# Written order for the first transform and the start of the first chunk

## The chip, the cores and the metric

One core of a Trainium2 chip runs the whole kernel as one program. The metric is the device time of one execution in microseconds. The core has five queues that matter here: TensorE (PE, with its weight loads as PEld), VectorE (DVE), ScalarE (ACT), GpSimd (POOL) and SyncE (SP), which only issues DMAs. Each executes its own instructions in order and waits on semaphores for the others.

## The reference

Eight sequences of 3072 tokens with 256 channels go through three stages:

```python
y = irfft(rfft(x, axis=1) * (filt_r + 1j*filt_i), n=3072, axis=1)
xk, xr = mix of y and y shifted by one token, with mu_k and mu_r
k = relu(xk @ w_k); v = (k*k) @ w_v; r = sigmoid(xr @ w_r); z = r * v
h = max(z @ w1, z @ w2, z @ w3); out = h @ w_out
```

The weights arrive as 64-bit floats. Most products are made from a high and a low part of each factor, as three matmuls.

## The kernel before

The long transform is cut in two factors, 48 x 64. `fft_first` does it for sequence 0, where nothing else is there to overlap with; `fft(b)` yields the pieces of the transform of sequence b, which `drive` mixes into the work of the sequence before. `fft_first` has two loops. Stage A (16 steps) multiplies x by `wa_f` and stores the result to `s1` in DRAM (`evac`, L474 and L475, on the SP queue). Stage B/C (12 steps, and two to drain) reads `s1` back (`x_load`), multiplies (tile `pb`), and makes two products with the filter (tile names in the profile: `filt` for the DVE product at L547, `q` for the POOL product at L544 from the half-swapped copy `v`, L542 and L543). Two steps later it multiplies again (`pc`) and stores to `s2` (L474, on the ACT queue). `w_double` copies halves of the matrices `wcr` and `wci` (L462, L463). The DVE product is written over the filter `f`, so it waits until POOL has read `f`.

`y_load(i)` reads one chunk of `s2` (a sequence has 8 chunks): tile `cin`, and `cprev` for the first. `y_mm(i)` finishes the inverse transform (`py`), copies it to `yt` and mixes it with the token before (`xm`, L606 on ACT and L607 on DVE), splits it in two parts (`xh`, `xl`), for `k` and `r`. `kv(i)` yields the units of one chunk: `k_mm` (`pk`), `v_mm` (`pv`, which takes `w_v` pieces of tile `ws` through `piece_of`), `r_mm`, and `y_load` and `y_mm` of the next chunk. After four chunks `second(0)` starts on w1, w2, w3 and w_out.

Weights are narrowed by jobs. `piece` gives each job a load (`wst`, three buffers, L201) and a narrowing: one ACT instruction (`we`, L212), five DVE instructions (L213 to L219) and a POOL addition (`wf`, L222). `parts` then makes the high part (DVE L231, or ACT L229 if `late`) and the low part (POOL L232). `wjobs1` holds nine jobs: 0 to 3 for `w_k`, 4 to 7 for `w_v` (their parts go to `wvd` in DRAM by a POOL-issued DMA, L273, and come back as `ws`), 8 for `w_r`. `wjobs2` holds twelve: nine for w1, w2 and w3, three for `w_out`; the nine have sums made by matmuls (`ps`), stored to `wud`. `pipelined` makes step k load job k+1, narrow job k and finish job k-2; these steps are inserted among the units of the first chunks.

What sets the order: a planner that estimates times puts the instructions of each engine in order, except inside `manual_schedule`, where the instructions of the named engines keep the order in which they are written among themselves. Instructions written outside of it may still be put ahead. Before the change SP keeps its order until `y_load(0)`, and ACT and PE for `fft_first`; DVE and POOL are left to the planner throughout. Jobs 0 to 4 are narrowed in `fft_first`, each whole at one step (`CONV`); jobs 5 to 8 are written behind `y_mm(0)`.

Of the kernel before, what the change touches and what calls it, by code (L numbers as in the profile page):

```python
# [9 lines left out]
F32 = mybir.dt.float32  # L10
F32R = mybir.dt.float32r
I32 = mybir.dt.int32
U32 = mybir.dt.uint32
# [112 lines left out]
def tile_spectral_moe(ctx: ExitStack, tc, x, filt, ones, wa, wa1, wi, wbc, wb1, wc1, filt1, filt0, mu, w_k, w_v, w_r, w1, w2, w3, w_out, out):  # L126
# [57 lines left out]
    def piece(src, kt, t0, t1, c0, c1, parts):  # L184

        wide = src.dtype != F32
        if wide:
            src = src.bitcast(I32)
        v = src.rearrange("(t p) n -> p t n", p=P)
        a, c = t1 - t0, c1 - c0  # L190
        st = {}

        def load(stage=None):
            if stage is not None:
                st["t"] = stage.rearrange("p (a n) -> p a n", a=a)
# [7 lines left out]
        def narrow(late=True):  # L203
            if not wide:
                st["r"] = st["t"]
                return
# [5 lines left out]
            nc.scalar.activation(ef, high.bitcast(F32), AF.Abs)  # L212
            nc.vector.tensor_scalar(ef, ef, as_float(0x38000000), as_float(0x47EFFFFF), op0=ALU.max, op1=ALU.min)  # L213
            nc.vector.tensor_scalar(e, e, 3, 0x3FFFFFFF, op0=ALU.logical_shift_left, op1=ALU.bitwise_and)
            nc.vector.scalar_tensor_tensor(e, high, -0x40000000, e, ALU.bitwise_and, ALU.bitwise_or)
            m = fp.tile([P, a, c], I32, tag="fin", name="wm")
            mf = m.bitcast(F32)
            nc.vector.tensor_scalar(m, e, -0x800000, None, op0=ALU.bitwise_and)
            nc.vector.scalar_tensor_tensor(mf, low.bitcast(U32), 2.0**-52, mf, ALU.mult, ALU.mult)  # L219
            cnt[0] += 1  # L220
            r = fp.tile([P, a, c], F32, tag=("flo", "fhi")[cnt[0] % 2], name="wf")
            nc.gpsimd.tensor_tensor(r, ef, mf, ALU.add)  # L222
            st["r"] = r

        return load, narrow, lambda late=True: parts(st["r"], late)

    def to_parts(hi, lo, r, late):
        if late:
# [194 lines left out]
    def fft_first(pp, jobs):  # L423
# [59 lines left out]
        xb = []  # L483

        def x_load(s):
# [24 lines left out]
        w_double(0)  # L510
        f_load(3)
        jobs[1][0]()
        x_load(1)
        wb_load(1)
        wc_load(1)
        f_load(4)
        jobs[2][0]()
        f_load(5)
        x_load(2)
        stage = pp.tile([P, 2, 1024 if wide else 512], I32 if wide else F32, tag="big", name="stage", bufs=4)  # L520
        jobs[3][0]()
        f_load(6)
        qs = {}
        for s in range(NG // 2 + 2):
            if 7 <= s + 4 < NG // 2:
                f_load(s + 4)
            if s == 4:
                wb_load(2)
                w_double(1)
            if s == 6:  # L530
                wc_load(2)
            if s in LOAD:
                jobs[LOAD[s]][0](*((stage[:, LOAD[s] - 4],) if LOAD[s] < 6 else ()))
            if s < NG // 2:
                p = ps.tile([NK, 2, C], F32, tag="pm", name="pb")
                for k in range(2):
                    g = 2 * s + k
                    mm(p[:, k], wt[g // LW][0][:, g % LW], xb[g // LX][:, g % LX], True, True)
                f = ft[s]
                q = pp.tile([NK, 2, C], F32, tag="q1", name="q1", bufs=3)  # L540
# [7 lines left out]
                qs[s] = q  # L548
            if s >= 2:
                f, q = ft[s - 2], qs[s - 2]  # L550
                p = ps.tile([NK, 2, C], F32, tag="pm", name="pc")
                for k in range(2):
                    g = 2 * (s - 2) + k
# [7 lines left out]
            if s == 8:  # L561
                w_double(2)

    first = ExitStack()
    first.enter_context(tc.manual_schedule(engines={mybir.EngineType.SP}))
# [303 lines left out]
    eye = mp.tile([P, 2, P], F32, tag="osb", name="eye")  # L869
    nc.sync.dma_start(eye, ones)  # L870
    for k in (5, 6, 7, 8):
        wjobs1[k][1]()
        wjobs1[k][2]()
    NPAIR = NTOT // 2
    units = kv(0) + kv(1) + kv(2) + [(0.0, lambda: combos(0))] + kv(3)
    marks, cuts = {}, {}
    before2 = len(units)
    s, left = second(0)
# [25 lines left out]
    lead = before2 + n2  # L904
    starts = [0] + [marks[b] + n2 for b in range(1, B)]
    ends = starts[1:] + [len(units)]
    for b in range(B):
        part = units[starts[b] : ends[b]]
        if b + 1 < B:
            side = fft(b + 1)  # L910
            cut = cuts[b] + n2 - starts[b]
            if b == 0:
                for _, fn in part[:lead]:
                    fn()
                part, cut = part[lead:], cut - lead
# [52 lines left out]
```

## Time and profile before

| | |
|---|---|
| Median of three runs | 3201.74 us (3200.74 to 3212.22) |
| Profiled execution, its own time | 3198.21 us |
| Its span | 3196.4 us |
| PE matmul busy | 3105.7 us (97%) |
| DVE, ACT, POOL busy | 1784.9, 1913.8, 1864.1 us |

Times below are microseconds from the start of the span of the profiled execution. The page cuts the span in 40 slices of 80 us; matmuls fill 6 and 7 tenths of the first two slices and 9 tenths or more of all from the third but the last. Everything that the change edits runs in the first three slices. PE busy time is modelled at the ends of matmuls, so small idle stretches are better read from the starts of instructions.

### The profile page before, as it was taken

To read this page: it belongs to the slowest core of one execution; us is meant where nothing else is said; L and a number is where in the kernel's file an instruction comes from. 1 tells how busy PE (TensorE), PEld (TensorE's weight loads), DVE (VectorE), ACT (ScalarE), POOL (GpSimd) and SP (SyncE) were. 2 spreads that over 40 slices of the span, in tenths; PEclk is the share of its full clock that TensorE was granted. 3 is DMA by queue.
4 is the path that set the end of the run, shared out by engine and by line. 5 is a ranking of instruction groups with operands and counts; after the bars stand their busy time and mean duration, and the time that the engine had idled before them with its cause. 6 is when DMAs were issued, how large, how long until landed. Compare 5 with 4: busy or idle time off the path is not lost.

```text
span 3196.4 us, 55749 instructions
## 1 busy us (share of the span) xinstructions
PE 3105.7 (97%) x19256; PEld 3031.7 (95%) x19256; DVE 1784.9 (56%) x2882; ACT 1913.8 (60%) x4024; POOL 1864.1 (58%) x1619
## 2 busy tenths in 40 slices
PE   6799999999999999999999999999999999999998
PEld 4789999999999999999999999999999999999998
DVE  4865564456554665456645466446664456555554
ACT  5556556656666566656666566665666566655554
POOL 3545675567655676546666566566665567544443
PEclk9899999999999999999999999999999999999999
DMA  8767796657766676757766577665876667555553
GB/s 292 234 227 226 235 329 192 195 181 247 246 197 184 213 241 211 215 173 234 257 198 186 178 259 252 198 191 165 269 249 189 190 195 245 182 170 160 166 168 122
DMA packets 397783, 676.38 MB, mean 212 GB/s; under 512 B 41920, under 2 KB 153664, under 8 KB 396864
## 3 DMA queue, kind: packets, MB, share of 16 engines
q1 hardware_dynamic: 328336, 585.61, 58.4%
q10 hardware_dynamic: 66752, 78.75, 7.2%
q0 software_dynamic: 2416, 8.46, 0.8%
q8 instruction: 156, 2.56, 0.3%
q14 instruction: 123, 1.01, 0.1%
HBM read 580.51 MB, written 92.14 MB: 210 GB/s over the span
## 4 chain that ended last, share of the span: by engine, by line
PE 84%; DMA 6%; DVE 5%; issue 2%; ACT 2%; POOL 1%; ACTq 0%; SPq 0%; POOLq 0%; DVEq 0%
PE pb L153 19%; PE pk L153 14%; PE pv L153 14%; PE po L153 12%; PE pe L153 9%; PE pa L153 7%; PE pr L153 4%; PE py L153 3%; DMA ws<-wud 3%; PE pc L153 2%; DVE xm L607 1%; DMA xb<-s 1%; PE ps L153 1%; DVE sc L665 1%; DVE m L748 1%
## 5 line engine op out<-in xcount | busy, mean ns | idle before, releaser
L153 PE MATMUL pb<-x,ws 128*128 128x384 f32 x3456 | 753.1, 338 | 23.0 <-DMA ws<-wud 16.9
L179 POOL TENSOR_TENSOR hh<-m,hh 128x384 fp32r<-128x384 f32 x384 | 402.2, 1056 | 522.4 <-ACT hh L178 426.3
L179 POOL TENSOR_TENSOR klo<-kr,khi 128x384 fp32r<-128x384 f32 x492 | 515.8, 1058 | 231.6 <-ACT khi L178 218.7
L153 PEld LDWEIGHTS pb<-x,ws 128*128 128x128 f32 x3456 | 598.7, 188 | 39.0 <-issue 15.2
L633 DVE SCALAR_TENSOR_TENSOR kr<-pk,kr 128x384 f32<-128x384 f32 x512 | 280.7, 553 | 444.9 <-ACT kr L632 443.6
L153 PE MATMUL po<-wo_hi,hh 128*128 128x256 f32 x2304 | 481.0, 283 | 3.1 <-ACT hh L178 1.6
L153 PE MATMUL pv<-khi,ws 128*128 128x384 f32 x2048 | 474.6, 337 | 4.0 <-ACT khi L178 4.0
L153 PEld LDWEIGHTS po<-wo_hi,hh 128*128 128x128 f32 x2304 | 389.9, 190 | 7.6 <-ACT hh L178 4.0
L153 PE MATMUL pe<-x,ws 128*128 128x384 f32 x1728 | 389.0, 337 | 0.6
L178 ACT CAST khi<-kr 128x384 fp32r<-128x384 f32 x512 | 260.2, 513 | 185.0 <-DVE kr L633 167.6
L153 PEld LDWEIGHTS pv<-khi,ws 128*128 128x128 f32 x2048 | 360.4, 188 | 7.0 <-ACT khi L178 5.3
L153 PE MATMUL pk<-xh,wk_hi 128*128 128x384 f32 x1024 | 341.4, 338 | 7.6 <-ACT xh L178 6.2
L153 PE MATMUL pk<-xl,wk_hi 128*128 128x384 f32 x1024 | 343.6, 336 | 0.9 <-DVE xl L179 0.9
L153 PE MATMUL pk<-xh,wk_lo 128*128 128x384 f32 x1024 | 343.4, 335 | 0.0
L153 PE MATMUL po<-wo_lo,hh 128*128 128x256 f32 x1152 | 316.6, 282 | 0.0
L632 ACT ACTIVATE kr<-pk 128x384 f32<-128x384 f32 x512 | 249.9, 490 | 109.0 <-POOL klo L179 48.7
L748 DVE TENSOR_TENSOR m<-sc,m 128x384 f32<-128x384 f32 x384 | 307.8, 806 | 9.2
L153 PEld LDWEIGHTS pe<-x,ws 128*128 128x128 f32 x1728 | 296.0, 188 | 3.1 <-PE pb L153 2.2
L153 PE MATMUL pv<-klo,ws 128*128 128x384 f32 x1024 | 292.3, 337 | 0.8 <-POOL klo L179 0.4
L179 POOL TENSOR_TENSOR xl<-xm,xh 128x768 fp32r<-128x768 f32 x126 | 233.4, 1869 | 89.7 <-ACT xh L178 89.7
L178 ACT CAST hh<-m 128x384 fp32r<-128x384 f32 x384 | 193.0, 514 | 134.2 <-DVE m L748 67.0
L607 DVE SCALAR_TENSOR_TENSOR xm<-yt,nmu_s,xm 128x384 f32<-128x384 f32 x256 | 180.1, 748 | 145.4 <-ACT xm L606 145.4
(129 smaller groups left out, 6028.0 us busy)
## 6 DMA issues: line engine op xcount, KB each, us to landing
ws<-wud SPq DMA_DIRECT2D x864, 256.0 KB, 3.5
ws<-wvd SPq DMA_DIRECT2D x512, 256.0 KB, 3.3
filt<-in_filt SPq DMA_DIRECT2D x84, 512.0 KB, 5.3
ws<-wud SPq DMA_DIRECT2D x288, 128.0 KB, 3.5
wbc<-wbcd SPq DMA_DIRECT2D x72, 512.0 KB, 5.4
cin<-s SPq DMA_DIRECT2D x64, 384.0 KB, 4.2
out_dram<-osb ACTq DMA_DIRECT2D x192, 128.0 KB, 3.1
xb<-s SPq DMA_DIRECT2D x85, 256.0 KB, 3.5
```

Source lines behind the costliest of these rows:

```text
L153: nc.tensor.matmul(o, lhsT=wgt, rhs=rhs, start=start, stop=stop, skip_group_check=more)
L178: nc.scalar.copy(hi, src)
L179: (lo_eng or nc.gpsimd).tensor_tensor(lo, src, hi.bitcast(F32), ALU.subtract)
L607: nc.vector.scalar_tensor_tensor(v[:, h], yt[:, h, :, :MC], nmu_s[:, w, h : h + 1], v[:, h], ALU.mult, ALU.add)
L632: nc.scalar.activation(r, p, AF.Relu)
L633: nc.vector.scalar_tensor_tensor(r, p, 0.0, r, ALU.max, ALU.mult)
L665: eng.tensor_tensor(t, a, b, ALU.subtract)
L748: nc.vector.tensor_tensor(m, c, m, ALU.max)
```

## The change

`piece` gains `steps`, a list of the single instructions of a narrowing with its parts as the last entry. `fft_first` collects such steps in `todo` and takes three of them (four from step 8 on) at the end of each step of stage B/C. The DVE product goes to a buffer of its own, `u`, instead of over `f`. `x_load(0)` moves ahead of the filter and `wc` loads; the loads of jobs 3 to 8 stand at steps 2 and 8 to 12. Jobs 5 and 6 are narrowed ahead of `y_load(0)`, jobs 7 and 8 behind `y_mm(0)`. ACT, PE, DVE and POOL keep the written order until then. The first eight `ws` loads (`piece_of(0)`) are written there, and SP keeps its written order until twelve units of the first chunks have been written.

```diff
-        CONV = {0: 1, 3: 2, 5: 3, 8: 4}
-        LOAD = {6: 4, 8: 5, 9: 6, 11: 7}
+        LOAD = {2: 3, 8: 4, 9: 5, 10: 6, 11: 7, 12: 8}
+        CONV = {2: 1, 5: 2, 8: 3, 11: 4}
...
+        def convert(n):
+            while todo and n:
+                todo.pop(0)()
+                n -= 1
...
-            if s == 4:
-                nc.sync.dma_start(f0, filt0)
-                f_load(0)
             if s == 6:
-                wc_load(0)
-                jobs[0][1](False)
-                jobs[0][2](False)
+                todo += jobs[0][3]()
+        convert(8)
+        x_load(0)
+        nc.sync.dma_start(f0, filt0)
+        f_load(0)
+        wc_load(0)
         f_load(1)
+        x_load(1)
+        jobs[1][0]()
         f_load(2)
-        x_load(0)
-        w_double(0)
...
+                nc.vector.scalar_tensor_tensor(u, p, sgn, f, ALU.mult, ALU.mult)
                 nc.scalar.copy(v[:H], p[H:])
                 nc.scalar.copy(v[H:], p[:H])
                 nc.gpsimd.tensor_tensor(q, v, f, ALU.mult)
-                nc.vector.scalar_tensor_tensor(f, p, sgn, f, ALU.mult, ALU.mult)
...
+            if s in (1, 4, 8):
+                w_double((1, 4, 8).index(s))
...
             if s in CONV:
-                k = CONV[s]
-                jobs[k][1](False)
-                jobs[k][2](False)
+                todo += jobs[CONV[s]][3]()
+            convert(3 if s < 8 else 4)
+        convert(len(todo))
...
-    with tc.tile_pool(name="pp", bufs=1) as pp, tc.manual_schedule(
-        engines={mybir.EngineType.Activation, mybir.EngineType.PE}
-    ):
+    start = ExitStack()
+    start.enter_context(tc.manual_schedule(engines={ET.Activation, ET.PE, ET.DVE, ET.Pool}))
+    with tc.tile_pool(name="pp", bufs=1) as pp:
         fft_first(pp, wjobs1)
...
+    for k in (5, 6):
+        for fn in wjobs1[k][3](True):
+            fn()
     y_load(0)
-    first.close()
...
-    wjobs1[8][0]()
     y_mm(0)
-    for k in (5, 6, 7, 8):
-        wjobs1[k][1]()
-        wjobs1[k][2]()
+    for k in (7, 8):
+        for fn in wjobs1[k][3](True):
+            fn()
+    chunk0 = kv(0)
+    piece_of(0)
+    start.close()
...
+    FIRST = 12
+    for _, fn in units[:FIRST]:
+        fn()
+    first.close()
```

## Rows read from the trace of the kernel before

**Rows 1.** Busy time by stage; in brackets instructions, then granted clock, DMA share, GB/s.

```profile
28.00:62.00 34.00, 22.40 (x84) 17.49 (x84) 15.14 (x21) 17.17 (x26) 15.01 (x12) 0.80 0.99 342
62.00:86.00 24.00, 17.46 (x70) 13.67 (x68) 20.11 (x27) 15.60 (x26) 17.30 (x13) 0.93 0.55 192
86.00:98.00 12.00, 0.00 (x0) 0.00 (x0) 11.48 (x15) 3.08 (x6) 8.54 (x8) 0.64 1.02 327
98.00:113.50 15.50, 10.26 (x37) 9.54 (x38) 15.29 (x26) 6.99 (x15) 5.13 (x4) 0.51 0.91 310
...
138.00:197.00 59.00, 57.72 (x397) 56.87 (x396) 50.78 (x78) 36.30 (x74) 30.46 (x24) 1.00 0.61 203
```

**Rows 2.** Chain of waits up to 130 us: start, duration, what.

```profile
33.29 11.17 DMA wb<-in_wb
44.47 10.16 DMA filt<-in_filt
...
76.98 1.40 DVE wm L218
```

**Rows 3.** Timeline of the SP queue: start, duration, line, transfer.

```profile
83.21 0.37 SPq L201 DMA_DIRECT2D wst<-in_w  x1
...
90.07 0.38 SPq L201 DMA_DIRECT2D wst<-in_w  x1
90.67 0.68 SPq L579 DMA_DIRECT2D cin<-s  x1
```

**Rows 4.** Timeline of stage B/C: its first and twelfth step, its last store.

```profile
34.78 2.05 PE L153 MATMUL pb<-xb,wb 128*128 128x256 f32 x4 [9.88 <-DMA xb<-s]
...
71.03 1.03 PE L153 MATMUL pb<-xb,wb 128*128 128x256 f32 x4
...
85.55 0.33 ACTq L475 DMA_DIRECT2D s<-e  x1
```

**Rows 5.** Groups of instructions by line and form, 28 to 86 us.

```profile
L544 POOL TENSOR_TENSOR q<-v,filt 128x512 f32<-128x512 f32 x12 | 16.7, 1394 | 22.2 <-ACT v L543 22.0
L547 DVE SCALAR_TENSOR_TENSOR filt<-pb,sgn,filt 128x512 f32<-128x512 f32 x12 | 8.9, 744 | 21.7 <-POOL q L544 21.7
L222 POOL TENSOR_TENSOR wf<-we,wm 128x512 f32<-128x512 f32 x6 | 8.1, 1349 | 3.8 <-DVE wm L219 3.8
L474 ACT COPY e<-pc 128x512 f32<-128x512 f32 x12 | 7.0, 585 | 7.0 <-PE pc L153 6.8
L542 ACT COPY v<-pb 64x512 f32<-64x512 f32 x12 | 7.0, 582 | 14.5 <-PE pb L153 7.1 <-PE pc L153 3.4 <-POOL wf L222 2.1
```

**Rows 6.** One tile's instructions up to 240 us: duration in ns, minimum/median/maximum.

```profile
L213 DVE TENSOR_SCALAR we<-we x21: 412/427/1351, 20.1 to 193.7; 128x512 f32<-128x512 f32 x21
L215 DVE SCALAR_TENSOR_TENSOR we<-wst,we x19: 676/691/1783, 21.0 to 196.1; 128x512 int32<-128x512 int32 x19
```

**Rows 7.** The page's DMA issues: count, KB each, median us to landing.

```profile
cin<-s SPq DMA_DIRECT2D x64, 384.0 KB, 4.2
```

**Rows 8.** DMA issues between 75 and 100 us.

```profile
wvd<-wvs POOLq DMA_DIRECT2D x4, 512.0 KB, 4.5
...
s<-e ACTq DMA_DIRECT2D x3, 256.0 KB, 4.7
```

**Rows 9.** Timeline from the first `py` to the first `pk`.

```profile
98.10 3.70 PE L153 MATMUL py<-wi_s,cin 96*128 96x96 f32 x16 [12.18 <-DMA eye<-in_ones]
...
105.71 3.21 DVE L607 SCALAR_TENSOR_TENSOR xm<-yt,nmu_s,xm 128x384 f32<-128x384 f32 x4
...
106.92 1.65 PE L153 MATMUL pk<-xh,wk_hi 128*128 128x384 f32 x4 [4.27 <-ACT xh L178]
```

**Rows 10.** Timeline of later narrowings and of the last `ps`.

```profile
134.47 0.43 DVE L213 TENSOR_SCALAR we<-we 128x512 f32<-128x512 f32 x1 [0.99 <-ACT we L212]
...
193.71 0.43 DVE L213 TENSOR_SCALAR we<-we 128x512 f32<-128x512 f32 x1 [3.10 <-ACT we L212]
...
210.24 1.72 PE L153 MATMUL ps<-wf,eye 128*128 128x128 f32 x14
```

More of the change, by code (lines that the diff above doesn't have):

```diff
@@ L201, in load, with steps @@
             nc.sync.dma_start(st["t"], v[:, t0:t1, k * c0 : k * c1])
-        def narrow(late=True):
+        def steps(late=False):
             if not wide:
                 st["r"] = st["t"]
-                return
+                return [lambda: parts(st["r"], late)]
             w = st["t"].rearrange("p a (n k) -> p a n k", k=2)
@@ L211, in narrow, with add, split_up @@
             ef = e.bitcast(F32)
[L212 to L215, printed above, removed]
             m = fp.tile([P, a, c], I32, tag="fin", name="wm")
             mf = m.bitcast(F32)
[L218 to L225, printed above, removed]
+            vec = nc.vector
+            def add():
+                cnt[0] += 1
+                r = fp.tile([P, a, c], F32, tag=("flo", "fhi")[cnt[0] % 2], name="wf")
+                nc.gpsimd.tensor_tensor(r, ef, mf, ALU.add)
+                st["r"] = r
+            return [
+                lambda: nc.scalar.activation(ef, high.bitcast(F32), AF.Abs),
+                lambda: vec.tensor_scalar(ef, ef, as_float(0x38000000), as_float(0x47EFFFFF), op0=ALU.max, op1=ALU.min),
+                lambda: vec.tensor_scalar(e, e, 3, 0x3FFFFFFF, op0=ALU.logical_shift_left, op1=ALU.bitwise_and),
+                lambda: vec.scalar_tensor_tensor(e, high, -0x40000000, e, ALU.bitwise_and, ALU.bitwise_or),
+                lambda: vec.tensor_scalar(m, e, -0x800000, None, op0=ALU.bitwise_and),
+                lambda: vec.scalar_tensor_tensor(mf, low.bitcast(U32), 2.0**-52, mf, ALU.mult, ALU.mult),
+                add,
+                lambda: parts(st["r"], late),
+            ]
+        def narrow():
+            for fn in steps()[:-1]:
+                fn()
+        def split_up(late=True):
+            if not wide:
+                st["r"] = st["t"]
+            parts(st["r"], late)
+        return load, narrow, split_up, steps
     def to_parts(hi, lo, r, late):
@@ L517, in fft_first @@
         jobs[2][0]()
+        x_load(2)
         f_load(5)
-        x_load(2)
+        f_load(6)
         stage = pp.tile([P, 2, 1024 if wide else 512], I32 if wide else F32, tag="big", name="stage", bufs=4)
-        jobs[3][0]()
-        f_load(6)
         qs = {}
@@ L528, in fft_first @@
                 wb_load(2)
-                w_double(1)
             if s == 6:
@@ L532, in fft_first @@
             if s in LOAD:
-                jobs[LOAD[s]][0](*((stage[:, LOAD[s] - 4],) if LOAD[s] < 6 else ()))
+                jobs[LOAD[s]][0](*((stage[:, LOAD[s] - 4],) if 4 <= LOAD[s] < 6 else ()))
             if s < NG // 2:
@@ L539, in fft_first @@
                 f = ft[s]
+                u = pp.tile([NK, 2, C], F32, tag="u1", name="u1", bufs=3)
                 q = pp.tile([NK, 2, C], F32, tag="q1", name="q1", bufs=3)
                 v = pp.tile([NK, 2, C], F32, tag="v1", name="v1", bufs=2)
+                nc.vector.scalar_tensor_tensor(u, p, sgn, f, ALU.mult, ALU.mult)
                 nc.scalar.copy(v[:H], p[H:])
@@ L546, in fft_first @@
                     nc.gpsimd.tensor_tensor(q[:H, 0], v[:H, 0], f0, ALU.mult)
[L547 to L548 removed]
+                qs[s] = u, q
+            if s in (1, 4, 8):
+                w_double((1, 4, 8).index(s))
             if s >= 2:
[L550 removed]
+                f, q = qs[s - 2]
                 p = ps.tile([NK, 2, C], F32, tag="pm", name="pc")
@@ L557, in fft_first @@
             if s in CONV:
-                k = CONV[s]
-                jobs[k][1](False)
-                jobs[k][2](False)
-            if s == 8:
-                w_double(2)
-    first = ExitStack()
-    first.enter_context(tc.manual_schedule(engines={mybir.EngineType.SP}))
-    with tc.tile_pool(name="pp", bufs=1) as pp, tc.manual_schedule(
-        engines={mybir.EngineType.Activation, mybir.EngineType.PE}
-    ):
+                todo += jobs[CONV[s]][3]()
+            convert(3 if s < 8 else 4)
+        convert(len(todo))
+    first = ExitStack()
+    ET = mybir.EngineType
+    first.enter_context(tc.manual_schedule(engines={ET.SP}))
+    start = ExitStack()
+    start.enter_context(tc.manual_schedule(engines={ET.Activation, ET.PE, ET.DVE, ET.Pool}))
+    with tc.tile_pool(name="pp", bufs=1) as pp:
         fft_first(pp, wjobs1)
@@ L858, in second @@
         return u, [(0.71, lambda q=q: o_mm(p, NU // 2 - 1, q)) for q in range(2 * NTB)]
+    for k in (5, 6):
+        for fn in wjobs1[k][3](True):
+            fn()
     y_load(0)
-    first.close()
+    eye = mp.tile([P, 2, P], F32, tag="osb", name="eye")
+    nc.sync.dma_start(eye, ones)
     for _ in range(8):
@@ L866, in tile_spectral_moe @@
         mm(p, wk[0][:, 0, :P], wk[0][:, 0, :NT], True, True)
-    wjobs1[8][0]()
     y_mm(0)
-    eye = mp.tile([P, 2, P], F32, tag="osb", name="eye")
-    nc.sync.dma_start(eye, ones)
-    for k in (5, 6, 7, 8):
-        wjobs1[k][1]()
-        wjobs1[k][2]()
+    for k in (7, 8):
[4 more added lines that the diff above has]
+    start.close()
     NPAIR = NTOT // 2
-    units = kv(0) + kv(1) + kv(2) + [(0.0, lambda: combos(0))] + kv(3)
+    units = chunk0 + kv(1) + kv(2) + [(0.0, lambda: combos(0))] + kv(3)
     marks, cuts = {}, {}
@@ L906, in tile_spectral_moe @@
     ends = starts[1:] + [len(units)]
+    FIRST = 12
+    for _, fn in units[:FIRST]:
+        fn()
+    first.close()
+    starts[0] = FIRST
     for b in range(B):
@@ L912, in tile_spectral_moe @@
             if b == 0:
-                for _, fn in part[:lead]:
+                for _, fn in part[: lead - FIRST]:
                     fn()
-                part, cut = part[lead:], cut - lead
+                part, cut = part[lead - FIRST :], cut - lead + FIRST
             drive(part[:cut], side, sum(w for w, _ in part[:cut]), sum(w for w, _ in side))
```

3 lines of the change are left out of this document (1 added, 2 removed).

## The prediction, made before the changed kernel was run

> **What bounds the kernel now.** I read the page's slices first: matmuls fill nine tenths of every slice from the third on, so the change can only move the moment at which that dense part begins, or disturb it. The table by stage comes next [rows 1]. From 28 to 62 us the DMA engines are full (share 0.99, 342 GB/s) while every compute engine has room: the first transform is bound by its loads there. The chain of waits agrees: it runs through a load of `wb` and one of `filt` [rows 2]. From 62 to 86 us the DMA share is 0.55 and DVE is busy 20.11 of 24 us [rows 1]; the chain now goes from one narrowing instruction to the next [rows 2], though what has to be finished is the transform. From 86 to 98 us PE does nothing and DVE is busy 11.48 of 12 us [rows 1]. The matmuls wait for `cin`, whose load is issued at 90.67 and whose result is used at 98.10 [rows 3, 9]. From 98 to 113.5 us the granted clock is 0.51, so TensorE runs at the lower of its two levels, after it had stood idle; from 138 us it is 1.00 and PE is busy 57.72 of 59 us [rows 1]. There DVE is the next engine, with 50.78 of 59.
>
> **The stage B/C loop.** Now it takes its first `pb` at 34.78, its twelfth at 71.03 and issues its last store at 85.55 [rows 4]: 36.25 us for eleven steps, 3.30 each, and a tail of 14.5 us.
>
> Ahead of `x_load(0)` go away `f0` (64 KB), one filter piece (256 KB) and the two halves of `wc` (256 KB each), 0.85 MB by their tile shapes. At 342 GB/s [rows 1] that is 2.5 us, so the first `pb` comes at about 32.3. The bounds are 0 and 2.5; I take the whole, because the queue is full there. The same bytes are behind it now, and steps 2 to 4 wait for them, so this alone would be worth less than 2.5 at the end of the loop.
>
> Per step ACT has three copies, 0.58 + 0.58 + 0.59 us [rows 5], and a store issue of 0.33 [rows 4]. My estimate for the ACT shares of four narrowings and of six `w_double` copies, spread over twelve steps, is 0.7; I took an ACT narrowing instruction like a copy of its size and a `w_double` copy, twice as wide, at twice that: (4 x 0.6 + 6 x 1.05) / 12. Sum 2.8 us. POOL has 1.39 for `q`, and per job 1.35 for the sum and about the same for the low part [rows 5], a third of that per step: 2.3 us. DVE has 0.74 for `u` [rows 5] and a third of a job: 3 x 0.43 + 2 x 0.69 for the narrowing [rows 6] and 0.43 for the high part, 3.1 per job, so 1.03 per step. The narrowing instructions take 0.43 alone and up to 1.35 when they meet POOL, those with two inputs 0.69 and up to 1.78 [rows 6]. If they and POOL never run together, the step takes 2.3 + 1.03 = 3.3 us. DMA gives a bound too: from `x_load(0)` to the last filter piece 12.7 MB have to pass (x 3.1, filter 3.2, `wb` 1.0, `wc` 1.6, jobs 1 to 3 1.6, eight stores 2.1), 37 us at 342 GB/s, hence a little over 3 us per step. I take 3.15, between 2.8 and 3.5: the twelfth `pb` at 32.3 + 11 x 3.15 = 67.
>
> The tail shortens for two reasons. Jobs 5 and 6 no longer stand between its instructions, and `u` needs no wait for `q`: the wait of `filt` for POOL, 21.7 us in this stretch [rows 5], goes. What is late next is `q`, which ACT feeds. From the last `pb`: 1.0 for it, 1.2 for two copies, 1.4 for `q`, 2.0 for `pc` (eight matmuls, where the four of `pb` take 1.03 [rows 4]), 0.6 for the copy and 0.5 to the issue, 6.7 us. The last store goes out at 73.7 instead of 85.55: **-12 us** (bounds: 2.8 per step gives -16, 3.5 and a tail of 8 gives -7).
>
> **From the last store to `py`.** Now 12.55 us (85.55 to 98.10) [rows 4, 9]. `cin` is issued 0.6 after a `wst` load that the planner had put ahead and that waited for a buffer [rows 3], and it then shares full DMA engines (1.02) [rows 1]. In the new order nothing of the second job list is ahead of it. The store may land in 3.5 us (median here 4.7 [rows 8]), `cin` and `cprev` take 1.4 to issue and 4.2 to land [rows 7]: 9.1 us, **-3.5** (bounds 0 and -5). The narrowing of jobs 5 and 6 is hidden in this stretch: two times 3.1 us of DVE and two times 2.7 of POOL in 9 us. Without that cover it would hold up `y_mm(0)` by the excess.
>
> **`y_mm(0)`.** DVE takes up `xm` at 105.71, 7.6 us after `py` [rows 9], because narrowings stood before it. In the written order it is free. But ACT and DVE then alternate for each half, where the planner had put four ACT instructions side by side. I expect the first half of `xh` 1 us sooner after `py`: **-1** (bounds -2 and +2).
>
> **What is given back.** Two things. First, `piece_of(0)` writes eight `ws` loads into SP's fixed order, and the last two need job 7, which is narrowed only behind `y_mm(0)`. SP stands in front of them, and behind it stand `cin` of the second chunk and the first loads of the second job list. From the start of `py`: 6 us to `xm` (7.6 now, less its delay), then four rounds of ACT 0.6, DVE 0.8 (3.21 for four [rows 9]) and ACT 0.6, 14 us to the end of `y_mm(0)`, then 0.7 ACT, 2.7 narrowing, 1.35 sum, 0.6 high part, 1.35 low part, 0.6 to issue, 4.5 to land [rows 8]: 26 us; `cin` at 31, its results some 10 us later. In the meantime PE has 124 matmuls of `k`, `v`, `r` and the next `py`, 18 us at 0.145 each (57.72 us for 397 [rows 1]) and some more at the lower clock, so from 8 to about 32 us; the first `ps` needs a narrowing that begins with that load at 31 and takes some 5. I count **+3** (bounds 0 and 8).
>
> A rule of the Trainium skill speaks against this place: SBUF — State Buffer, section "SBUF: two separate sides", says that a DMA issued from POOL cannot write its descriptors while DVE holds the shared port, and gives 0.62 us alone and 3.1 overlapped. Job 8's DVE instructions would then add 2.5 us to job 7's store, and the sum by it would be 2.5 us longer. The median landing of 4.5 us [rows 8], with DVE nearly always busy [rows 1], holds that already or doesn't show it.
>
> Second, the pre-work of DVE is lost. Six of the twelve jobs of the second list are narrowed before 134 us (the seventh begins at 134.47, the twelfth at 193.71 [rows 10]), mostly while PE stood idle. Now their loads come after `cin` of the second chunk, so about five narrowings, 5 x 2.7 = 13 us of DVE, move into the dense part, where DVE has 8.2 us free in 59 [rows 1]: **+5** (bounds 0, if they slip behind the fourth chunk, and 13).
>
> **Sum.** -12 - 3.5 - 1 + 3 + 5 = -8.5 us on the profiled 3198.21: 3189.7. The median of the runs lies 3.5 us above the profiled execution, which gives 3193.
>
> **Rivals.**
> *The front counts in full.* PE fills the waits in chunk 0 with other units, and the jobs slip into the stretch after the fourth chunk. For it: the `ps` matmuls are what has to be on time, and the narrowings are now two jobs ahead of them. Against: DVE busy 50.78 of 59 [rows 1]. It gives -16.5: 3185.
> *DVE carries all of it over.* DVE is idle only 0.7 us from 86 to 113.5 [rows 1], so what ends this part is the sum of its work, and a front that is shorter on PE only moves that work. Against: what it did there was not due yet. It gives 0 to -1: 3201.
> *The second stage waits for its weights: slower.* The narrowings go at one per 11.85 us from 134.47 to 193.71 [rows 10]. The first in_w job now lands at about 83 + 31 = 114; the ninth job's `ps`, two steps after its narrowing, would come at 114 + 10 x 11.85 = 232 instead of 210 [rows 10]. Nothing else is there to be multiplied before `second(0)`. Price: 22 us over today's time, 3224. It decides if the pace stays above 9.6 us per job; from there down it costs nothing. Against it: DVE can go faster once chunks leave room.
>
> **How the numbers follow.** Forecast 0.47, front in full 0.26, carried over 0.18, second stage late 0.09. A difference of 0.5%, 16 us, is about what a measurement of this kernel tells from no change, so faster means under 3185.7 and slower over 3217.8. Half of the second case and an eighth of the first lie below: 0.20. The last case gives slower: 0.09. The range takes the better bounds of the loop (-16) with no give-back down to about 3181, and on the other side give-backs of 8 and 13 with a loop of -7, which come to +8: 3210.
>
> **What would show it.** Right: last store at 70 to 79 us, `py` 8 to 10 us after it, first `pk` 14 to 18 us earlier than 106.92, no `wst<-in_w` load ahead of `cin`, SP waiting before the seventh `ws` load, narrowings of the second list later than now with DVE above 90% in the dense part. Wrong: a loop step still at 3.3 us with a long tail, a last `ps` well after 211, or the gain of the front still standing at 250 us.

## The result, and the profile after

The changed kernel takes 3227.37 us (median of four runs, 3222.68 to 3228.66) where the kernel before takes 3201.81: a ratio of 1.0075, 95% interval 1.0063 to 1.0087. It is slower by 25.6 us; 3193 was forecast, with a range up to 3210. The profiled span is 3225.6 us, 29.2 more than before. In these two executions the whole of that is lost before the second stage begins: its first product with the weights (`pb<-x,ws`, called PB2 from here on) starts at 254.34 us, at 225.35 before, 29.0 later; 2971 us follow it in both.

The busy time by stage comes first, in the columns of [rows 1]: PE, PEld, DVE, ACT, POOL, then granted clock, DMA share, GB/s.

```profile
28.00:62.00 34.00, 23.06 (x74) 16.81 (x74) 8.06 (x14) 12.18 (x19) 12.29 (x10) 0.72 0.97 323
62.00:86.00 24.00, 16.48 (x55) 11.97 (x56) 9.49 (x18) 11.95 (x20) 11.11 (x9) 0.86 0.53 178
86.00:98.00 12.00, 6.76 (x24) 5.27 (x24) 5.86 (x10) 5.90 (x10) 6.29 (x6) 0.86 0.24 92
98.00:113.50 15.50, 7.71 (x30) 7.50 (x31) 7.38 (x13) 5.85 (x13) 6.65 (x8) 0.51 0.61 211
113.50:140.00 26.50, 15.43 (x71) 13.80 (x70) 15.44 (x29) 11.34 (x23) 5.64 (x5) 0.76 0.50 175
140.00:180.00 40.00, 37.58 (x236) 35.63 (x235) 39.60 (x60) 24.05 (x48) 20.31 (x16) 0.97 0.67 204
```

The reader is to look down the DVE column. From 28 to 98 us DVE worked 46.73 us before [rows 1] and 23.41 now. Nothing took over: from 62 to 98 us the DMA share and all engines have room. From 140 us DVE then has 39.60 of 40 us: it works off there what it did not do in the front. What that costs PE is worked out with f1 below.

The timeline of stage B/C (start, duration, engine, line, tiles), as in [rows 4]:

```profile
31.22 2.05 PE L153 MATMUL pb<-xb,wb 128*128 128x256 f32 x4 [7.12 <-issue]
...
79.07 1.91 PE L153 MATMUL pb<-xb,wb 128*128 128x256 f32 x4
...
93.91 0.33 ACTq L492 DMA_DIRECT2D s<-e  x1
```

The loop starts 3.6 us sooner, but a step takes (79.07 - 31.22) / 11 = 4.35 us, and the tail is 14.8. Why is in the waits of ACT, DVE and POOL from 28 to 86 us (waiting instruction, what released it, us in total, times, longest):

```profile
ACT v L563 <- DVE u L562: 26.8, 9, 11.7
...
DVE wk_hi L248 <- POOL wf L219: 13.8, 4, 5.7
DVE u L562 <- DMA filt<-in_filt: 11.4, 3, 6.2
...
POOL q L565 <- ACT v L564: 25.7, 9, 6.8
```

One step of the loop in the timelines of POOL, DVE and ACT:

```profile
70.13 1.27 POOL L565 TENSOR_TENSOR q<-v,filt 128x512 f32<-128x512 f32 x1 [0.87 <-ACT v L564]
71.36 1.26 POOL L219 TENSOR_TENSOR wf<-we,wm 128x512 f32<-128x512 f32 x1
...
72.65 0.43 DVE L248 CAST wk_hi<-wf 128x512 fp32r<-128x512 f32 x1 [3.86 <-POOL wf L219]
73.00 0.74 DVE L562 SCALAR_TENSOR_TENSOR u<-pb,sgn,filt 128x512 f32<-128x512 f32 x1
...
73.83 0.58 ACT L563 COPY v<-pb 64x512 f32<-64x512 f32 x1 [3.17 <-DVE u L562]
```

These rows form a ring. `q` of one step keeps POOL from the sum of a weight job; DVE stands in front of that job's high part and waits for the sum; `u` of the next step stands behind it; `v` on ACT waits for `u` (both read `pb`, and `u` is written first); and the next `q` waits for `v`. Each engine is idle for somebody's place in the written order. DVE's 17.55 us of work from 28 to 86 us is no limit. Besides, `u` needs a filter piece, which `v` did not, and these pieces now come behind `x` (11.4 us).

The SP queue behind the loop (start, duration of the group, line, transfer, count), as in [rows 3]:

```profile
99.48 0.33 SPq L600 DMA_DIRECT2D cin<-s  x1
99.86 0.47 SPq L604 DMA_DIRECT2D cprev<-s  x1
100.38 0.42 SPq L887 DMA_DIRECT2D eye<-in_ones  x1
100.85 28.34 SPq L282 DMA_DIRECT2D ws<-wvd  x8
129.28 0.38 SPq L600 DMA_DIRECT2D cin<-s  x1
129.77 0.93 SPq L201 DMA_DIRECT2D wst<-in_w  x2
```

Eight `ws` loads take 28.34 us because the seventh waits for job 7's store, which POOL issues at 125.45. Behind them stand `cin` of the second chunk (102.32 before) and all loads of the second job list. PE then has nothing:

```profile
125.96 0.62 PE L153 MATMUL pv<-klo,ws 128*128 128x384 f32 x2 [0.17 <-DVE klo L179]
135.56 2.85 PE L153 MATMUL py<-wi_s,cin 96*128 96x96 f32 x12 [8.98 <-DMA cin<-s]
```

The first and the twelfth narrowing of the second list, and the last `ps` (93.04, 193.71 and 219.10 before):

```profile
137.32 0.43 DVE L224 TENSOR_SCALAR we<-we 128x512 f32<-128x512 f32 x1 [9.16 <-ACT we L223]
...
222.82 0.43 DVE L224 TENSOR_SCALAR we<-we 128x512 f32<-128x512 f32 x1 [1.87 <-ACT we L223]
...
248.10 1.17 PE L153 MATMUL ps<-wf,eye 128*128 128x128 f32 x9
```

The first is 44 us late, the twelfth and the last `ps` 29. So the narrowings regain 15 us of their late start, and the rest goes through to the end.

### The profile page after: what moved, and what is told of

Read it like the earlier page. It is cut to its first block, busy times and chain, and to the rows that moved or that the text cites. A ratio compares the mean times of both kernels' runs of the same rounds, so it can differ in the third digit from the quotient of the medians.

```text
span 3225.6 us, 55759 instructions
## 1 busy us (share of the span) xinstructions
PE 3122.3 (97%) x19256; PEld 3043.1 (94%) x19256; DVE 1777.0 (55%) x2882; ACT 1911.6 (59%) x4024; POOL 1861.4 (58%) x1619
## 4 chain that ended last, share of the span: by engine, by line
PE 82%; DMA 4%; DVE 4%; ACT 1%; issue 1%; POOL 1%; ACTq 0%; SPq 0%; POOLq 0%; DVEq 0%
PE pb L153 19%; PE pk L153 14%; PE pv L153 14%; PE po L153 12%; PE pe L153 9%; PE pa L153 6%; PE pr L153 4%; PE py L153 3%; DMA ws<-wud 3%; PE pc L153 1%; DMA xb<-s 1%; DVE xm L628 1%; DVE sc L686 1%; DVE m L769 0%; DMA s<-ao 0%
## 5 line engine op out<-in xcount | busy, mean ns | idle before, releaser
L153 PE MATMUL pb<-x,ws 128*128 128x384 f32 x3456 | 753.8, 338 | 22.5 <-DMA ws<-wud 16.5
```

Of the source, the lines that this page charges most:

```text
L153: nc.tensor.matmul(o, lhsT=wgt, rhs=rhs, start=start, stop=stop, skip_group_check=more)
```

## The experiments

Three theories stood against each other. **Chain:** the written order makes the loop slow. **Block:** SP's order behind the first `cin` holds up the second chunk. **DVE's sum:** what has to be done on DVE in front of the second stage is a fixed sum, and idle time that DVE has in the front comes back at its end, whatever PE gains. The table has all runs; each ratio is to the kernel before on the same chip (medians 3199.04 for e1 to e4, 3199.19 for e5 to e8, 3199.93 for f, 3203.14 for g). "DVE idle" is the length less DVE's busy time from 28 to 113.5 us in the view of the first fence. The last four columns are from one profiled execution each. Behind PB2 these executions take between 2969 and 2983 us, so time and PB2 need not move by the same amount. "Thin" kernels leave out the first DVE instruction of a narrowing in the second list; their twelfth narrowing is given by the next one, which starts 0.46 us after the first in before and after.

| kernel | median us | ratio (95%) | first `pk` | DVE idle | 12th narrowing | PB2 |
|---|---|---|---|---|---|---|
| before | 3201.81 | | 106.92 | 23.5 | 193.71 | 225.35 |
| after | 3227.37 | 1.0075 (1.0063-1.0087) | 110.34 | 54.7 | 222.82 | 254.34 |
| e1 no early `ws` | 3221.17 | 1.0067 (1.0051-1.0084) | 108.31 | 53.5 | 212.18 | 245.09 |
| e2 `u` last | 3219.61 | 1.0062 (1.0047-1.0077) | 100.08 | 42.9 | 211.56 | 242.99 |
| e3 new front only | 3214.23 | 1.0049 (1.0034-1.0064) | 111.75 | 43.8 | 207.59 | 239.41 |
| e4 new back only | 3213.71 | 1.0047 (1.0032-1.0062) | 96.16 | 36.5 | 206.37 | 239.32 |
| e5 SP free | 3216.07 | 1.0054 (1.0039-1.0069) | 109.38 | 53.7 | 210.47 | 243.56 |
| e6 SP free, `u` last | 3205.96 | 1.0025 (1.0013-1.0037) | 100.09 | 40.9 | 201.01 | 233.84 |
| e7 before, SP written | 3201.27 | 1.0009 (0.9999-1.0018) | 100.28 | 29.2 | 193.75 | 226.68 |
| e8 `y` first | 3200.59 | 1.0003 (0.9993-1.0012) | 103.07 | 30.2 | 196.28 | 229.52 |
| f1 after, thin list 2 | 3212.58 | 1.0051 (1.0033-1.0069) | 109.02 | 53.6 | 209.31 | 239.13 |
| f2 before, thin list 2 | 3197.64 | 0.9991 (0.9979-1.0003) | 105.46 | 24.6 | 189.96 | 220.29 |
| f3 e7, thin list 2 | 3194.76 | 0.9987 (0.9976-0.9999) | 102.78 | 33.6 | 191.29 | 222.12 |
| f4 front planned | 3214.18 | 1.0048 (1.0033-1.0063) | 95.30 | 35.3 | 206.55 | 238.14 |
| g1 front planned, old back | 3203.86 | 0.9999 (0.9989-1.0009) | 98.01 | 27.6 | 195.42 | 228.59 |
| g2 front planned, `y` first | 3204.46 | 1.0011 (1.0000-1.0022) | 99.50 | 29.3 | 195.38 | 228.60 |
| g3 as g1, `u` last | 3205.18 | 1.0008 (0.9999-1.0017) | 99.35 | 28.1 | 197.03 | 228.67 |

**e1, no early `ws` loads.**

```diff
     chunk0 = kv(0)
-    piece_of(0)
```

> The changed kernel without the call that writes the first eight ws loads ahead of the second chunk's cin; they are written when the first v_mm asks for them. Theory (SP stands in front of the seventh ws load until job 7's parts have landed, and the second cin and the second job list's loads stand behind it): the second cin is issued right behind the first py, near 107 instead of 129.3, the second py starts near 120 instead of 135.6, and the median falls by 12 to 20 us from 3227, to 3207 to 3215. Rival (the lost pre-work of DVE alone is the cause; PE only waits there because DVE is late): the second cin comes early too, but the first product of the second stage stays within 5 us of 268.2 and the median at 3222 to 3227.

The second `cin` goes out at 105.48, but PE only gets its next `py` at 127.83 and PB2 comes at 245.09: neither theory's numbers (the 268.2 in the text was read from a later row; the PB2 of after is 254.34). The block had moved:

```profile
105.89 13.29 SPq L201 DMA_DIRECT2D wst<-in_w  x2
119.23 2.83 SPq L282 DMA_DIRECT2D ws<-wvd  x6
```

Now a `wst` load waits for a buffer that job 7 still reads, and the `ws` loads stand behind it. One call was taken out of the fixed order, not the fixed order; e5 is the clean test.

**e2, `u` behind `v` and `q`.**

```diff
-                nc.vector.scalar_tensor_tensor(u, p, sgn, f, ALU.mult, ALU.mult)
                 nc.scalar.copy(v[:H], p[H:])
...
+                nc.vector.scalar_tensor_tensor(u, p, sgn, f, ALU.mult, ALU.mult)
```

> The changed kernel with the DVE product u written behind the two copies v and the product q instead of ahead of them; its own buffer stays. Theory (the copies on ACT wait for u on DVE, which stands behind narrowing instructions that wait for POOL, which stands behind q: one chain through three engines per step): a step of stage B/C takes 3.3 to 3.6 us instead of 4.35, the last store goes out near 85 instead of 93.9, and the median falls by 5 to 9 us, to 3218 to 3222. Rival (the step is paced by the loads, or by POOL and DVE sharing time): the last store stays within 2 us of 93.9 and the median at 3225 to 3229.

The step falls from 4.35 to 3.67 us, the last store from 93.91 to 85.27, `pk` comes 10.3 us sooner; in the same waits of ACT the row of `v` for `u` is gone and `v` waits for `pb` (12.7 us). So the place of `u` in the written order cost the front some 9 us. The second `cin` still goes out 28 us behind the first `ws` load (118.86), so the block is there as before, but it has moved forward with the front: PB2 falls by 11.4 us. The median lies 20.6 us above before instead of 25.6.

**e3 and e4, each half alone.** e3 has the new `fft_first` and the old back, e4 the reverse:

```diff
-    start.enter_context(tc.manual_schedule(engines={ET.Activation, ET.PE, ET.DVE, ET.Pool}))
     with tc.tile_pool(name="pp", bufs=1) as pp:
         fft_first(pp, wjobs1)      # e3: the changed one, e4: the one of before
+    start.close()                  # e3: here; e4: start is entered here
```

> Only the front of the change: the new stage B/C loop with its loads, steps and fixed order on four engines; behind it everything as before (jobs 5 to 8 behind y_mm(0) in the planner's order, no early ws loads, SP fixed only until the first cin). Theory (three causes: loop about 8 us at its last store, SP block about 15, late narrowings about 11): 3 to 10 us slower than before, 3205 to 3212. Rival (the front is not what costs, since the later cin wait gives it back): within 3 us of before.

> Only the back of the change: the loop of stage B/C, its loads and its narrowings as before, DVE and POOL free there; then jobs 5 and 6 ahead of the first cin, 7 and 8 behind y_mm(0), all in fixed order, the early ws loads, and SP fixed for twelve units. Theory: the SP block and the late narrowings are here, 14 to 26 us slower than before, 3216 to 3228. Rival (front and back only cost together): under 8 us slower, below 3210.

(The edits are shortened.) By the medians e3 costs 15.2 us, where 3 to 10 were expected, and e4 14.7, at the lower end of 14 to 26; the change, which has both, costs 25.6. Two losses that nearly add up (at PB2 14.1, 14.0 and 29.0). In e4 `pk` comes 10.8 us sooner than before (jobs 7 and 8 and the list-2 loads are no longer ahead), and PB2 is 14 us later all the same.

**e5 and e6, SP planned from the identity load on; then `u` last as well.**

```diff
     nc.sync.dma_start(eye, ones)
+    first.close()
...
-    FIRST = 12
-    for _, fn in units[:FIRST]:
-        fn()
-    first.close()
+    FIRST = 0
```

> The changed kernel, but SP keeps the written order only as far as the first chunk's cin and the identity load; from there the planner places its issues, the eight early ws loads too. Theory A (SP's queue: the seventh ws load, which waits for job 7's store, holds up the second chunk's cin and all list-2 loads for 28 us, and this starts the late narrowings): second cin issued before 110 us instead of 129.28, second py before 124 instead of 135.56, list-2's first narrowing before 118 instead of 137.32, first narrowed product of the second stage (PB2) 240 to 245 instead of 254.34, time 3209 to 3214. Theory B (job 7 and job 8 stand too late, and DVE, full from then on, sets the pace whatever SP does): second cin earlier, but PB2 stays above 250 and the time at 3218 or more.

> As e5, and u stands behind v and q in the first transform's loop, as in e2. Theory A (two independent losses, the loop's chain and SP's queue): last store at about 85, PB2 229 to 234, time 3199 to 3204, no difference from the kernel before. Theory B (DVE's narrowings are the last to end, what is won ahead of them is waited out there): PB2 within 4 us of e5's, time within 4 us of e5's.

The SP timeline of e5, where the planner puts the second `cin` between the `ws` loads:

```profile
100.01 0.91 SPq L282 DMA_DIRECT2D ws<-wvd  x2
104.53 0.38 SPq L201 DMA_DIRECT2D wst<-in_w  x1
107.09 0.80 SPq L282 DMA_DIRECT2D ws<-wvd  x2
107.98 0.38 SPq L600 DMA_DIRECT2D cin<-s  x1
114.29 0.79 SPq L282 DMA_DIRECT2D ws<-wvd  x2
```

PB2 falls by 10.8 us (254.34 to 243.56) and with `u` last by 9.7 more (to 233.84), both inside theory A's numbers; the list-2 narrowings began later than it said (125.39 in e5), and the times, 3216 and 3206, lie 2 us above its ranges. By the medians, each against its own before, e5 regains 8.7 us of 25.6 and e6 18.8. Both losses are shown to be real, and at PB2 their two gains nearly add up (11.4 for `u` alone, 10.8 for SP alone, 20.5 for both). 8.5 us of PB2 and a ratio of 1.0025 are left, which neither explains.

**e7 and e8, the kernel before with single parts of the change.** e7 only keeps SP in the written order for twelve units, so that list-2 loads no longer go ahead of the second `cin`. e8 has jobs 5 and 6 ahead of `cin` and a fixed order through `y_mm(0)`; the loads of the identity and of job 8 stand earlier too.

```diff
     y_load(0)
-    first.close()                  # e7
...
+    FIRST = 12                     # e7
+    for _, fn in units[:FIRST]:
+        fn()
+    first.close()
```

```diff
+    for k in (5, 6):               # e8
+        for fn in wjobs1[k][3](True):
+            fn()
     y_load(0)
...
     y_mm(0)
+    start.close()
+    first.close()
```

> The kernel before with one thing of the change: SP keeps the written order for the first twelve units of the chunks too, so that the list-2 loads no longer go ahead of the second chunk's cin; DVE, ACT, POOL and the loop are planned as before, and no ws load is put ahead. Theory A (the loss needs the early ws loads or the fixed order on DVE): PB2 within 4 us of 225.35, time 3197 to 3204. Theory B (the pre-work of DVE that is lost from 86 to 134 us is by itself what makes the second stage late): first list-2 narrowing after 105 instead of 93.04, PB2 236 to 242, time 3210 to 3216.

> The front of the kernel before; jobs 5 and 6 stand ahead of cin, all engines keep the written order through the first chunk's y products and no further; no early ws loads, jobs 7 and 8 and all later loads are left to the planner. Theory A (the early pk of e4, 10 us ahead of before, is kept if SP and DVE are free behind it): pk at 95 to 98 as in e4, second cin before 104, PB2 214 to 220, time 3189 to 3194. Theory B (what is done earlier on PE is waited out at the narrowings of the second list, because DVE has the same sum of work in front of the second stage): pk early, PB2 within 4 us of 225.35, time 3197 to 3203.

Both bring `pk` forward (6.6 and 3.9 us) and both take as long as the kernel before. In e7 the first list-2 narrowing comes at 105.06 instead of 93.04, and the twelfth at 193.75 where it was at 193.71: the lost pre-work is caught up, but the earlier start of PE is gone too. So e7 went as its theory A had it: 5.7 us of pre-work lost by itself costs nothing, because DVE had idle time behind 113.5 us to take it up (13.1 us before, 7.5 in e7). e8 went as its theory B, by 0.2 us more in PB2.

**f1 and f2, less work for DVE.** In the second list's narrowing two of five DVE instructions, the clamp of the exponent and the product with the low half, are left out in the changed kernel and in the one before (f2 by a flag, to the same effect).

```diff
-            for fn in steps()[:-1]:
-                fn()
+            for n, fn in enumerate(steps()[:-1]):
+                if n not in (1, 5):
+                    fn()
```

> The changed kernel, where the narrowing of the second job list leaves out two of its five DVE instructions (the clamp of the exponent and the product with the low half; the second stage's weights are then not the reference's). By the profile of after these are 12 x (0.52 + 0.75) = 15 us of DVE in front of the second stage. Theory A (from about 140 us on DVE's sum of work ends last, so the time DVE stood idle in the front comes back one for one): first product of the second stage (PB2) 236 to 242 instead of 254.34, time 3207 to 3213. Theory B (the second stage is late because its loads begin late, or because TensorE runs at its lower level after each idle stretch): PB2 within 5 us of 254.34, time above 3217.

> The kernel before with the same two DVE instructions left out of the second list, some 16 us of DVE. Theory A (there PE and DVE are both full from 113 to 190 us and end together): less than half of it shows, PB2 217 to 225 instead of 225.35, time 3191 to 3199. Theory B (DVE alone sets the pace there too): PB2 208 to 213, time 3183 to 3188.

In the changed kernel PB2 falls by 15.2 us, about the whole of the work removed, and the median lies 12.7 us above that of before instead of 25.6; DVE's busy time up to the twelfth narrowing falls by 16.4 (122.97 to 106.59). From 140 to 180 us, f1, the columns as above:

```profile
140.00:180.00 40.00, 37.52 (x251) 36.41 (x250) 33.99 (x53) 26.21 (x51) 24.05 (x17) 1.00 0.80 253
```

In the kernel before, the same removal moves PB2 by 5.1 us and the time by too little to tell (0.9979 to 1.0003): there PE is full as well.

What DVE's full stretch costs PE, and what it does not, is in the view from 140 us to PB2, for before, after, f1 and f2 (in this order):

```profile
140.00:225.35 85.35, 81.59 (x555) 80.42 (x553) 62.08 (x98) 47.81 (x98) 40.82 (x33) 1.00 0.61 201
140.00:254.34 114.34, 103.46 (x654) 100.61 (x654) 92.63 (x141) 61.62 (x124) 55.83 (x43) 0.94 0.63 203
140.00:239.13 99.13, 95.73 (x642) 93.92 (x641) 73.80 (x115) 59.16 (x119) 53.03 (x41) 1.00 0.70 229
140.00:220.29 80.29, 78.81 (x534) 78.11 (x533) 52.59 (x84) 45.94 (x94) 39.17 (x32) 1.00 0.63 207
```

The first count in brackets is the matmuls that PE still has ahead of it at 140 us; from 28 us to PB2 there are 904 or 905 in all four. Before needs 85.35 / 555 = 0.154 us for each, after 0.175, f1 0.154 again. So some 14 us of the 29.0 (654 x 0.021) are lost behind 140 us, where DVE is full up to 200, and f1 regains them. The other 15 (99 matmuls more, at 0.154) had been lost by 140 us, and f1 has them still: its front is as slow as that of after, its second `cin` as late (128.11), its PB2 18.8 us behind that of f2 and its median 14.9. In e3 nearly all of the loss is of this second kind: 641 matmuls are left at 140 us, and from there to 180 PE is busy for 39.97 of 40 us at a clock of 1.00. So DVE's fullness behind 140 us is shown to cost about half of the loss. The other half is there by 140 us, and these runs do not say what share DVE has in it.

**f3, e7 with the thin list.**

> e7 (SP in the written order for twelve units, its pk 6.6 us sooner than before, its time the same) with the same two DVE instructions left out. Theory A (e7's earlier front was given back because DVE had no room behind it): now the front shows, PB2 5 to 8 us below that of f2, time 4 to 8 us below f2's. Theory B (it was given back on PE or at the loads): PB2 within 2 us of f2's.

Not decided: the planner moved `pk` to 102.78, 2.7 us ahead of f2's 105.46 instead of 6.6, and DVE idles 33.6 us in the front. PB2 came 1.8 us after f2's, which is B's number, and the median 2.9 us below f2's, which is neither's, but the early front that was to be tested was hardly there.

**f4, the changed kernel with DVE and POOL planned in `fft_first`.**

```diff
-    start.enter_context(tc.manual_schedule(engines={ET.Activation, ET.PE, ET.DVE, ET.Pool}))
-    with tc.tile_pool(name="pp", bufs=1) as pp:
+    with tc.tile_pool(name="pp", bufs=1) as pp, tc.manual_schedule(engines={ET.Activation, ET.PE}):
         fft_first(pp, wjobs1)
+    start.enter_context(tc.manual_schedule(engines={ET.Activation, ET.PE, ET.DVE, ET.Pool}))
```

> The changed kernel, but in the first transform DVE and POOL are placed by the planner, as in the kernel before (u is still written ahead of v and q); from the narrowing of jobs 5 and 6 on the written order holds on all engines as in the change. Theory A (it is the place of u ahead of v in the program that makes v wait for DVE, whoever orders DVE): step of the loop 3.9 us or more, last pb at 75 or later, time 3219 to 3229. Theory B (it is the written order on DVE and POOL, in which u and q stand behind waiting conversions): step at most 3.5 us, last pb before 72, last store before 86.5, time 3211 to 3217 as in e4.

The last `pb`, the last store and the first `pk`, and SP's block behind them:

```profile
68.97 0.59 PE L153 MATMUL pb<-xb,wb 128*128 128x256 f32 x2
...
79.05 0.33 ACTq L492 DMA_DIRECT2D s<-e  x1
...
95.30 1.65 PE L153 MATMUL pk<-xh,wk_hi 128*128 128x384 f32 x4 [2.79 <-ACT xh L178]
```

```profile
92.83 21.16 SPq L282 DMA_DIRECT2D ws<-wvd  x8
114.08 0.38 SPq L600 DMA_DIRECT2D cin<-s  x1
```

Theory B in every number: the step is (68.97 - 31.03) / 11 = 3.45 us and `pk` 15 us sooner than in after. So the order of loads, the `u` tile and the single steps are good for the front; it is the written order on DVE and POOL that spoils it, where `u` stands behind waiting conversions. g3 says the same from the other side, since under the planner `u` last only makes the loop slower.

**g1, g2, g3: that front without the block.** g1 has the back of the kernel before; g2 that of e8; g3 is g1 with `u` last.

```diff
     fft_first(pp, wjobs1)          # planned as in f4
...
-    for k in (5, 6):               # g1; g2 keeps them and closes both orders behind y_mm(0)
-        for fn in wjobs1[k][3](True):
-            fn()
+    start.close()
     y_load(0)
+    first.close()
```

> The changed kernel's order of loads, its u tile and its conversions in single steps in the first transform, with DVE and POOL placed by the planner; everything behind the first transform as in the kernel before. Theory A (the front of f4 is real and worth its time where nothing blocks SP): last store near 79, pk 95 to 99, PB2 214 to 220 instead of 225.35, time 3189 to 3195. Theory B (what ends the stretch in front of the second stage is DVE's sum of work, and idle time that DVE has in the front is paid at its end): pk early all the same, PB2 223 to 230, time 3197 to 3204.

> f4 without its block: no early ws loads, SP planned from the identity load on, the written order on the engines closed behind the first chunk's y products. Theory A: pk 94 to 97 as in f4, PB2 213 to 220, time 3188 to 3195. Theory B: pk as early, PB2 223 to 232, time 3197 to 3206, with DVE idle for 7 us or more between 86 and 113.5 us.

> g1 with u written behind v and q, as in the kernel before. If the wait of v for u costs the loop something under the planner as well (13.3 us of ACT's idle time in f4), last pb comes 2 us or more sooner than in g1 and the last store before 78; the end moves by as much under theory A and by less than 2 us under theory B. If not, all marks lie within 2 us of g1's.

Theory B in the times and in PB2: in g1 the last store is 6.9 us sooner, `pk` 8.9, and PB2 stands at 228.59, 228.60 and 228.67, the times as before or up to 0.2% above. (DVE did not idle in g2 from 86 to 113.5 us as expected, 2.6 us; its idle time lies ahead of 86.) In g3 the last `pb` comes 3.9 us later than in g1, not sooner, so `v`'s wait for `u` costs nothing once DVE can take `u` at once.

The same loss seen from DVE is in one view, DVE from 28 us to its twelfth narrowing of the second list, before, after and g1 (in this order):

```profile
28.00:193.71 165.71, 129.12 (x722) 118.92 (x723) 129.15 (x193) 95.21 (x176) 83.59 (x65) 0.88 0.74 248
```

```profile
28.00:222.82 194.82, 144.34 (x725) 127.71 (x726) 122.97 (x197) 94.72 (x177) 84.28 (x67) 0.83 0.64 213
```

```profile
28.00:195.42 167.42, 130.66 (x722) 120.25 (x723) 132.18 (x196) 93.66 (x176) 89.46 (x67) 0.87 0.74 247
```

Some 195 instructions and 123 to 133 us of DVE work are done by then in all three, and in the other complete kernels too. What differs is DVE's idle time: 36.6, 71.8 and 35.2 us. Before, the planner filled the front with whatever DVE could do, due or not (idle for 0.7 us from 86 to 113.5); the change sends DVE through the front in order and leaves it idle for 31 us more there. g1's PE starts 9 us sooner, but DVE is idle as long as before, and PE waits later: between its first `pk` and `pv`, 5.0 us for `khi`, while ACT and DVE alternate between narrowings and the chunk. That DVE's sum is what makes it wait there is argued from these rows; no run that relieved DVE had such a front.

The idle time in the front does not set the end alone. e1 and e5 leave DVE idle there for as long as the change does (53.5 and 53.7 us), and their twelfth narrowing comes 10.6 and 12.4 us sooner than its; behind 113.5 us DVE idles for 17.2 us in after and for 5.6 in e5.

No complete version tried here beats the kernel before; five of them (e7, e8, g1 to g3) lie within 0.25% of it.

## Why the prediction was wrong

It failed at two steps, **"The stage B/C loop"** and **"What is given back"**. Up to the first `pk` 16.5 us were to be won, and 3.4 were lost (110.34 against 106.92); behind it 8 were to be given back, and 25.6 were.

*First `pb`*: 32.3 forecast, 31.22 found. 3.6 us were won, more than the upper bound of 2.5. The working counted one filter piece that goes from ahead of `x_load(0)`; by the diff three go (`f_load(0)` to `f_load(2)`), 1.38 MB in all by the same tile shapes and 4.0 us at 342 GB/s.

*The step of 3.15 us, the tail of 6.7, -12 us.* Found: 4.35, 14.8 and +8.4. The working added up busy times per engine and took the largest, as if order did not matter; the bounds, 2.8 to 3.5, were sums of the same kind. The sentence that failed is "`u` needs no wait for `q` [...]. What is late next is `q`, which ACT feeds." What was late next was `v`, which waits for `u`, which in a written order waits behind conversions. With DVE and POOL planned (f4) the step is 3.45 us, inside the bounds, and the last store comes at 79.05, -6.5 us where -12 was forecast: the tail is 10.1, not 6.7.

*Last store to `py`*: 9.1 forecast, 9.43 found, but not by the forecast way. The store landed 2 to 3 us after its issue, and then `cin` waited for job 5:

```profile
98.59 0.69 DVE L228 SCALAR_TENSOR_TENSOR wm<-stage,wm 128x512 f32<-128x512 uint32 x1
```

The `cin` row waits 5.2 us for this reader of `stage`, a tile of the pool that has just been closed; some 3 of them lie behind the last store's landing (issued at 93.91, 2.3 us). I had called the narrowing of jobs 5 and 6 hidden here; it was the last to end.

*`y_mm(0)`*: -1 forecast, -1.8 found; `py` to `pk` takes 7.0 us instead of 8.8.

*SP's block, +3 (0 to 8)*: its mechanism was right, its price too low. The working has job 7's store landed 26 us after the start of `py` and `cin` at 31, with no term for the 5 us between; `cin` went out 25.9 us after it, right behind the landing. The price was 10.8 us of PB2 (e5 against after) and 8.7 in the medians, above the bound. PE was said to have work until 32 us after `py`; it ran dry 23 us after it and stood still for 9, and its clock then stayed below full (0.76 from 113.5 to 140 us).

The store whose delay I had weighed by the Trainium skill (SBUF — State Buffer, section "SBUF: two separate sides") was issued in 0.57 us while DVE narrowed job 8 (124.46 to 128.16), and these stores landed in 3.3 us by their median, against 4.5 [rows 8]; the 2.5 us that would follow from that rule do not show here.

*DVE's pre-work, +5 (0 to 13)*: mis-sized. It counted five narrowings that move. In fact DVE left 31.2 us more idle up to 113.5 us, narrowings of both lists. e7 shows that idle time behind 113.5 us can take up a part of such a loss for nothing; in the changed kernel SP's block made DVE idle there as well (11.1 of 26.5 us up to 140), and from 140 us DVE was full, which cost PE some 14 us (f1). This and the loop have one source: the same written order that slows the loop keeps DVE from doing later work in the gaps.

*The rivals.* "The second stage waits for its weights" had the sign, the place and almost the number (3224 for 3227), at a chance of 0.09. Its working was not what happened: the first load landed 15 us or more after the forecast 114, and the narrowings then ran at (222.82 - 137.32) / 11 = 7.8 us, below the 9.6 from which it was to cost nothing. Of the 29 us some 14 came because DVE was full and the chunks' own work on it waited, the others because PE was behind by then. It also took the last `ps` from a row of the eighth group [rows 10]; the ninth starts at 219.10, and is 29.0 us later now. "DVE carries all of it over", at 0.18, came nearest to the rule for a faster front: e7, e8 and g1 to g3 have a first `pk` that is 4 to 9 us sooner and worth nothing. I drew from it that the change costs nothing; it also says that idle time added to DVE in the front has to be made up behind it, and there was room for a part of it only.

The upper end of the range does not follow from its own terms: give-backs of 8 and 13 with a loop of -7, -3.5 and -1 come to +9.5, not to +8.

What stays open: in the kernel before PE is full from 113.5 to 193.7 us (79.01 of 80.21) and DVE nearly so (67.12), and how much of an earlier front would show if DVE were relieved was not settled (f3). Nor was it separated how much of the loss up to 140 us is TensorE's lower granted clock (0.76 from 113.5 to 140 us in after, 1.00 in before) and how much is waiting.

## What to carry to other kernels

A written order has to be judged by each instruction's place in its queue, not by busy sums: for each instruction that another engine waits for, list what stands ahead of it and what that waits for. Where an engine has a fixed sum of work before some point, look for the idle time that a change adds to it; work that is not due yet but fills gaps is worth its length as soon as it is more than the idle time behind it can take up. Count also how far the engine that ends last is behind at that point: relieving the full engine gives back only what is lost from there on. A load that waits for a semaphore holds up everything behind it in its queue, so it does not belong ahead of loads that are ready.

## What the runs showed of the hardware

Two engines that only read the same PSUM tile waited for each other in the written order: ACT's copies of `pb` waited 26.8 us in all for DVE's product, and with the order turned round (e2) DVE waited for ACT, 4.1 us. A load into memory that a closed pool had used waited for the last reader of that pool's tile (5.2 us ahead of `cin`). The stores to `s` landed in a median of 2.0 us from 75 to 135 us in after, where DMA moved 135 GB/s, against 4.7 from 75 to 100 in before [rows 8], where it moved 237. And DVE's work is not quite a constant: about as many instructions (197 and 193) took 122.97 us in after and 129.15 in before; why was not looked into.
